# A fused forward and backward kernel on one core: value products placed earlier in the forward chain, and another order of loads and half chunks in the tail

## The chip, the cores and the metric

The kernel runs on one core of a Trainium2 chip. A core has a matrix engine (PE, with weight loads listed apart as PEld), VectorE (DVE), ScalarE (ACT), GpSimd (POOL) and SyncE (SP); each takes its own instructions in order, and they meet through semaphores. DMAs are issued from SP and from POOL. The metric is the device time of one execution in microseconds, as a median of several runs. The profile is one more execution, recorded instruction by instruction.

## The reference

The reference runs a transformer block forward and then takes the gradients of everything against a given `grad_out`. The attention goes through 64 segments of 32 tokens in turn. Each segment has 8 memory rows in front, which are the first 8 output rows of the segment before it:

```python
for s in range(n_seg):
    h = jnp.concatenate([mem, xs], axis=1)
    q, k, v = (einsum('btd,dhe->bhte', h, W) for W in (Wq, Wk, Wv))
    p = softmax(where(mask, q @ k.T * scale, -1e9))
    o = einsum('bhte,hed->btd', p @ v, Wo)
    mem = o[:, :M]
    outs.append(o[:, M:])
h = x + attention(layernorm(x)); out = h + (silu(hn @ Wg) * (hn @ Wu)) @ Wd
```

There are 2048 tokens of width 448, 16 heads of 256, and a hidden width of 1792. The outputs are `out` and the gradients of `x`, of the first memory, of Wq, Wk, Wv and Wo, and of the three weights of the gated layer. The memory makes the forward pass a recurrence over segments, and the backward pass one in the other direction.

## The kernel before

The kernel has four stages, one after the other: `forward_chain` (lines 359 to 810), `ffn_phase` (813), `backward_chain` (1032) and `tail_phase` (1289). They share a few large buffers in on-chip memory (`W`, `A`, `B`), cut by hand into tiles, so that a tile of one stage comes free only when the stage before has read it for the last time. PSUM has eight banks: five that go round under one name (`psf` in the profile), two (`fx`) and one (`po`, used as `ph` in the tail).

The order of instructions on an engine is made by a planner. It takes an instruction that it believes to be ready, those of higher rank first, and rank follows the order of the code. Code inside `k.prio.crit()` ranks above the rest. `tc.issue_after(x)` places an instruction behind `x` on its own engine. So an instruction that is written later can stand earlier in an engine's queue if, by the planner's reckoning, nothing of higher rank was ready there.

**A segment of the forward chain.** Queries and keys come first (`qk_rows`, L535 and L539, and their transposes, L549), then the scores of two halves of the heads (L622, L628) with a softmax each (L635 to L642 on DVE, the exponential on ACT, L637). Values are made in four banks. `value_rows(b)` (L652) does the three full chunks of the contraction for a bank, and `value_rest(b0)` (L660) does the last half chunk for two banks and copies both to on-chip memory, for the second pair one by ACT and one by DVE, the latter behind the end of the second softmax. `transposed_p(b)` (L671) turns the probabilities of half `b` and copies them. `values(b)` (L684) multiplies values and probabilities; its first four heads' columns are copied by DVE and the others by ACT, the token columns to `xblk` and then the memory columns. `out_proj` (L697) sums over all 32 column blocks in the bank `po`; the memory rows of the next segment come out of it (L728 to L738). `values(0)` reads the value banks 0 and 1, `values(1)` banks 2 and 3. `rest_unit` (L464) is work for later segments, laid behind `out_proj` in most segments.

**The tail.** It computes the weight gradients as sums over token blocks: 16 blocks of 128 tokens and, for the attention, 4 blocks with memory rows, 20 in all. For the gradient of Wo (`rows_by_d`, L1397) it goes through the blocks in the order 16 to 19 and then 15 down to 0. The stationary side is `X_o` (a tile a block, loaded by `outs(i0, i1, c0, c1)` for the blocks at places `i0` to `i1` of that order and the columns `c0` to `c1`), the moving side is `DCt`, gathered by `grads`. `grads(0)` issues four loads for the memory blocks (L342) and eight for the rest (L346, L347), and `grads(1)` four more (L349). `grads(0)` and the first `outs` are issued on SP in the last segment of the backward chain.

Then follow the gradients of Wv, Wk and Wq, in two halves each: six calls of `att`, and after the first and the third of them an `up_grad` for the two up-projections (16 blocks). Each makes two passes of `d_by_e` over its blocks, with seven accumulating banks: six for the three full chunks of the 448 rows (L1375), and one for the last 64 rows (the half chunks, L1380), which go to the two halves of the array by turns. With `frees` true the half chunks come after every four blocks; with `frees` false, in the first pass, all come at the end of the pass. In the first pass of `att` the four memory blocks are made on the way: a fetch from `M_v`, `M_k` or `M_q` on POOL (L1340), a pack by DVE and ACT (L1345, L1347), and a turn by PE (L1354) with copies. `k.last_mm` is the PE instruction behind which such a turn is placed. The last product (gradient of the down-projection) reads `GO`, a copy of `grad_out` that POOL loads (L1471) to the place where `DCt` and then `HN` lay before.

Of the kernel before, what the change touches and what calls it, by code (L numbers as in the profile page):

```python
# [15 lines left out]
P = 128  # L16
# [297 lines left out]
class _TailLoads:  # L314
# [18 lines left out]
    def grads(self, part):  # L333
        k, D, S, NT, M, SEG = self.k, self.k.D, self.k.S, self.k.NT, self.k.M, self.k.SEG
        sync, DHb = k.nc.sync, k.dr["DHb"]
        dcx = DHb[0:S, 0:D].rearrange("(t r i) d -> r i t d", r=4, i=SEG)
        dcm = DHb[S:, 0:D].rearrange("(t r m) d -> r m t d", r=4, m=M)
        dc8 = DHb[0:S, 0:D].rearrange("(g s i) d -> g s i d", s=16, i=SEG)
        if part == 0:
            for g in range(k.NB - NT):  # L340
                with k.tc.issue_after(k.last_load.ins):
                    sync.dma_start(out=self.DCt[:, NT + g], in_=dc8[g, :, 0:M])  # L342
        for r in range(4):
            if part == 0:
                with k.tc.issue_after(k.last_load.ins):
                    sync.dma_start(out=self.DCt[32 * r:32 * r + 24, :NT], in_=dcx[r, M:SEG])  # L346
                    sync.dma_start(out=self.DCt[32 * r + 24:32 * r + 32, 4:NT], in_=dcm[r, :, 4:NT])  # L347
            else:
                sync.dma_start(out=self.DCt[32 * r + 24:32 * r + 32, 0:4], in_=dcm[r, :, 0:4])  # L349
# [9 lines left out]
def forward_chain(k: _K):  # L359
    nc, tc = k.nc, k.tc  # L360
# [246 lines left out]
    for s in range(NSEG):  # L607
# [9 lines left out]
        with k.prio.crit():  # L617
# [29 lines left out]
            def value_rows(b):  # L647
                pV[b] = k.ps1()
                for kc in range(KC - 1):
                    for g in range(2):  # L650
                        n = 4 * g + b
                        nc.tensor.matmul(pV[b][64 * g:64 * g + 64, 0:512], lhsT=hT_flat[:, kc, sl * L:sl * L + 64],  # L652
                                         rhs=Wv_sb[:, kc, n * 512:(n + 1) * 512],
                                         start=(kc == 0), stop=False, skip_group_check=True)

            def value_rest(b0, held=None):
                for g in range(2):
                    for e in range(2):
                        m = 2 * g + b0 // 2
                        nc.tensor.matmul(pV[b0 + e][64 * g:64 * g + 64, 0:512], lhsT=hT_flat[64 * e:64 * e + 64, KC - 1, sl * L:sl * L + 64],  # L660
                                         rhs=Wv3[64 * e:64 * e + 64, m * 512:(m + 1) * 512],
                                         start=False, stop=True, skip_group_check=True)
                for e in range(2):
                    with tc.issue_after(held.ins) if held is not None and e == 1 else nullcontext():
                        k.evac(Vs[:, (b0 + e) * 512:(b0 + e + 1) * 512], pV[b0 + e][:, 0:512], "s" if held is None else "sv"[e])
# [11 lines left out]
            def values(b):  # L677
                for x in range(2):
                    po = k.ps1()
                    for hh in range(2):  # L680
                        h = HB * b + 2 * x + hh
                        for dc in range(DC):
                            i = 2 * hh + dc
                            nc.tensor.matmul(po[:, i * 2 * L:(i + 1) * 2 * L], lhsT=Vs[:, (2 * h + dc) * P:(2 * h + dc + 1) * P],  # L684
                                             rhs=PT_bd[:, h, :, :].rearrange("p g n -> p (g n)"), start=True, stop=True)
                    v = po[:, 0:8 * L].rearrange("p (j n) -> p j n", n=L)
                    j0 = 16 * b + 8 * x
                    k.evac(xblk[:, j0:j0 + 8, r * SEG:(r + 1) * SEG], v[:, :, M:L], "vs"[x])
                    k.evac(orr[:, j0:j0 + 8, :], v[:, :, 0:M], "vs"[x])
# [24 lines left out]
            value_rows(2)  # L714
            transposed_p(0)
            value_rows(3)
            value_rest(2, p_in)
            if end:
                k.fl.at(1)
            values(0)  # L720
            transposed_p(1)
            out_proj(0, 8)
            values(1)
# [308 lines left out]
def backward_chain(k: _K):  # L1032
# [98 lines left out]
    for s in range(NSEG - 1, -1, -1):  # L1131
# [12 lines left out]
        with k.prio.crit():  # L1144
# [25 lines left out]
                                         start=(dc == 0), stop=(dc == DC - 1), skip_group_check=True)  # L1170
            if s == 0:
                k.tl.grads(0)
                k.tl.outs(0, 7, 0, 6)
            pD3 = pD[:, 0:8 * L].rearrange("p (h n) -> p h n", n=L)
            prod = k.f32("f2", 8 * L, "prod")[:].rearrange("p (h n) -> p h n", n=L)
            nc.vector.scalar_tensor_tensor(out=prod, in0=pD3, scalar=k.scale, in1=P_sb, op0=ALU.mult, op1=ALU.mult)
# [112 lines left out]
def tail_phase(k: _K):  # L1289
# [72 lines left out]
    tl.outs(0, NB, 11, 16)  # L1362
    xo = tl.x

    def d_by_e(lhs_of, rhs_of, nblk, widths, store, at=None, frees=True):

        pa = accs(7)
        for b0 in range(0, nblk, 4):
            for fn in (at or {}).get(b0, ()):
                fn()  # L1370
            for b in range(b0, min(nblk, b0 + 4)):
                for kc in range(KC - 1):
                    for g in range(2):
                        w = widths[g]
                        k.last_mm = nc.tensor.matmul(pa[2 * kc + g][:, 0:w], lhsT=lhs_of(b)[:, kc * P:(kc + 1) * P], rhs=rhs_of(b, g),  # L1375
                                         start=(b == 0), stop=(b == nblk - 1), skip_group_check=True)
            for b in range(b0, min(nblk, b0 + 4)) if frees else range(nblk) if b0 + 4 >= nblk else ():
                for g in range(2):
                    w = widths[g]
                    k.last_mm = nc.tensor.matmul(pa[6][64 * g:64 * g + 64, 0:w], lhsT=lhs_of(b)[:, (KC - 1) * P:D], rhs=rhs_of(b, g),  # L1380
                                     start=(b == 0), stop=(b == nblk - 1), skip_group_check=True)
        for i in range(6):
            kc, g = divmod(i, 2)
            res = resbuf()
            evac(res[:, 0:widths[g]], pa[i][:, 0:widths[g]])
            store(kc, g, res[:, 0:widths[g]])
        res = resbuf()
        for g in range(2):
            evac(res[64 * g:64 * g + 64, 0:widths[g]], pa[6][64 * g:64 * g + 64, 0:widths[g]])
            store(KC - 1, g, res[64 * g:64 * g + 64, 0:widths[g]])  # L1390
# [29 lines left out]
    def att(hi, mem, after):  # L1420
        nm, oi, hf = halves[hi]
        o2 = OUT[oi].rearrange("d h e -> d (h e)")
        xt = load_x(nm, hf)
        for g in range(NG):
            xt[NT + g] = ring()
        for q in range(2):
            at = {}
            if q == 0:
                (f0, p0, t0), (f1, p1, t1), (f2, p2, t2), (f3, p3, t3) = mem
                at = {0: [p0, f2], 4: [lambda: t0(xt[NT]), p1, f3], 8: [lambda: t1(xt[NT + 1]), p2],  # L1430
                      12: [lambda: t2(xt[NT + 2]), p3], 16: [lambda: t3(xt[NT + 3])]}
            elif after is not None:
                at = {12: [after[0][0], after[1][0]]}

            def st(kc, g, r, q=q, hf=hf, o2=o2):
                e0 = (16 * g + 8 * hf + 4 * q) * P
                nc.gpsimd.dma_start(out=o2[kc * P:min(D, (kc + 1) * P), e0:e0 + 512], in_=r)  # L1437

            def rhs(b, g, q=q, xt=xt):
                return xt[b].rearrange("p (cl g n) -> p cl g n", g=2, n=P)[:, 4 * q:4 * q + 4, g, :]  # L1440
            d_by_e(lambda b: HC[:, b, :], rhs, NB, (512, 512), st, at, q == 1)

    def up_grad(nm, oi, after):
        xt = []
        for t in range(NT):
            x_t = ring()
            nc.sync.dma_start(out=x_t[:, 0:F], in_=dr[nm][t * P:(t + 1) * P, :])
            xt.append(x_t)
        for p0 in (0, 1024):
            ws = (512, min(512, F - p0 - 512))  # L1450

            def st(kc, g, r, p0=p0, oi=oi):
                f0 = p0 + 512 * g
                nc.gpsimd.dma_start(out=OUT[oi][kc * P:min(D, (kc + 1) * P), f0:f0 + r.shape[-1]], in_=r)

            def rhs(b, g, p0=p0, ws=ws, xt=xt):
                return xt[b][:, p0 + 512 * g:p0 + 512 * g + ws[g]]
            d_by_e(lambda b: HN[:, b, :], rhs, NT, ws, st, {8: [after[0][0], after[1][0]]} if p0 else None, p0 > 0)

    mems = [load_m(nm, hf) for (nm, _, hf) in halves] + [None]  # L1460
    mems[0][0][0]()
# [1 line left out]
    for hi in range(len(halves)):  # L1463
        att(hi, mems[hi], mems[hi + 1] if hi not in (0, 2) else None)
        if hi == 0:
            nc.gpsimd.dma_start(out=HN[:, 0:NT, :], in_=dr["HN"].rearrange("(t p) d -> p t d", p=P))
            up_grad("DGP", 7, mems[1])
        if hi == 2:
            up_grad("DU", 8, mems[3])
            GO = W(0, NB, D)  # L1470
            nc.gpsimd.dma_start(out=GO[:, 0:NT, :], in_=GO2.rearrange("(t p) d -> p t d", p=P))  # L1471

# [44 lines left out]
```

## Time and profile before

| What | Value |
|---|---|
| Median of 4 runs | 3096.22 us (3091.14 to 3101.26) |
| Profiled execution, its own time | 3088.07 us |
| Its span | 3086.3 us |
| PE busy | 2900.9 us, 94% of the span |
| DVE, ACT, POOL busy | 43%, 36%, 22% |
| PE busy from 0 to 1031.6 us (forward) | 933.7 of 1031.6 us |
| PE busy from 2399.9 us to the end (tail) | 653.1 of 686.4 us |
| Granted PE clock, mean | 0.991 |

In a timeline a row gives the start in microseconds from the start of the span, the duration, the engine, the line, the operation with the tile that it writes and the tiles that it reads, and the number of like instructions merged. In square brackets stands the time that the engine had been idle, and what it had waited for. A line number can be that of a helper: every copy out of PSUM is L75 (DVE) or L76 (ACT), and is told apart by its tiles and shape. Durations of matmuls overlap, so a rate is better read from the starts.

### The profile page before, as it was taken

What the parts mean: (1) busy time and instruction counts of PE and PEld (TensorE: products, weight loads), DVE (VectorE), ACT (ScalarE), POOL (GpSimd) and SP (SyncE); (2) the same over time, 40 slices, a digit from 0 to 9 for tenths busy, and PEclk for the clock granted to TensorE, in tenths of its full rate; (3) what the DMA queues carried; (4) which work ended last, traced back from release to release, by engine and by line L of the source; (5) the groups of instructions that cost most, each with busy time, mean ns of one, the idle gap of its engine ahead of it and who ended that gap; (6) DMA issues with size and microseconds to landing.
All of it is one profiled execution on the core that took longest, in us unless ns stands there. A gap on an engine that the chain in (4) does not pass through costs nothing.

```text
span 3086.3 us, 108337 instructions
## 1 busy us (share of the span) xinstructions
PE 2900.9 (94%) x47640; PEld 1737.6 (56%) x47650; DVE 1332.0 (43%) x3381; ACT 1114.9 (36%) x2634; POOL 673.3 (22%) x1507
## 2 busy tenths in 40 slices
PE   5899999999998999989999999999999899999999
PEld 3555555555554556666666666666666454444444
DVE  4555555555555577744444444444444001111110
ACT  2444444444444445433444344434444011111110
POOL 2222222222222222421221112212212111212111
PEclk9999999999999999989999999999999899999999
DMA  7566766766766999874554445545545998969951
GB/s 244 136 170 180 183 166 174 187 170 174 191 178 184 286 221 228 222 273 122 154 136 136 133 138 134 154 129 147 132 131 148 295 261 229 187 187 219 177 162 51
DMA packets 739468, 550.12 MB, mean 178 GB/s; under 512 B 600052, under 2 KB 635364, under 8 KB 736564
## 3 DMA queue, kind: packets, MB, share of 16 engines
q1 hardware_dynamic: 687956, 389.65, 51.8%
q0 software_dynamic: 51040, 153.54, 14.9%
q8 instruction: 374, 6.13, 0.8%
q14 instruction: 98, 0.80, 0.1%
HBM read 168.01 MB, written 234.23 MB: 130 GB/s over the span
## 4 chain that ended last, share of the span: by engine, by line
PE 65%; issue 15%; DMA 7%; DVE 6%; ACT 3%; POOL 3%; SPq 1%; POOLq 0%; ACTq 0%; DVEq 0%
PE po L1200 7%; PE psf L1151 7%; PE psf L535 6%; PE psf L652 5%; PE po L697 4%; PE psf L890 4%; PE psf L1128 4%; PE fx L1264 3%; PE fx L464 2%; PE fx L1014 2%; PE psf L1222 2%; DVE arA L75 2%; PE psf L549 2%; PE psf L1160 2%; PE psf L1397 2%
## 5 line engine op out<-in xcount | busy, mean ns | idle before, releaser
L75 DVE CAST arA<-psf 128x256 bf16<-128x256 f32 (+3 forms) x933 | 427.8, 479 | 782.4 <-PE psf L1375 233.6
L76 ACT CAST arA<-psf 128x96 bf16<-128x96 f32 (+5 forms) x915 | 353.4, 409 | 1011.5 <-PE psf L1375 254.7
L1200 PE MATMUL po<-arW,arA 128*32 128x448 bf16 x6144 | 347.8, 356 | 4.2 <-DMA arW<-Tq 2.7
L1375 PE MATMUL psf<-arW,arA 128*128 128x512 bf16 x980 | 249.6, 382 | 0.0
L1375 PEld LDWEIGHTS <-arA 128*128 128x128 bf16 x1440 | 137.0, 98 | 167.1 <-issue 18.0
L1151 PEld LDWEIGHTS <-arW 128*128 128x128 bf16 x8192 | 213.2, 96 | 24.8 <-issue 24.8
L1151 PE MATMUL psf<-arA,arW 128*128 128x40 bf16 x8192 | 216.6, 180 | 6.2 <-DVE arA L1226 5.1
L1200 PEld LDWEIGHTS <-arA 128*32 128x32 bf16 x6144 | 152.1, 96 | 115.7 <-ACT arA L76 9.2
L652 PE MATMUL psf<-arW,arA 128*64 128x512 bf16 x1536 | 216.4, 382 | 0.0
L535 PE MATMUL psf<-arW,arA 128*32 128x512 bf16 x3072 | 192.5, 383 | 12.5 <-DVE arA L738 12.5
L76 ACT CAST arB<-psf 128x64 bf16<-128x64 f32 (+3 forms) x384 | 122.0, 318 | 151.3 <-PE psf L539 108.1
L697 PE MATMUL po<-arW,arA 128*32 128x256 bf16 (+1 forms) x4096 | 141.3, 263 | 10.9 <-DVE arA L75 7.7
L890 PE MATMUL psf<-arW 128*128 128x256 bf16 (+1 forms) x1288 | 146.3, 274 | 1.3 <-DVE arA L956 0.7
L890 PEld LDWEIGHTS <-arW 128*128 128x128 bf16 (+1 forms) x1344 | 102.4, 97 | 51.5 <-issue 40.8
L1397 PE MATMUL psf<-arW 128*128 128x448 bf16 x525 | 113.2, 358 | 11.7 <-DMA arW<-X_o 11.7
L1161 ACT COPY arA<-psf 128x1024 bf16<-128x1024 bf16 x128 | 123.3, 1015 | 1.8 <-PE psf L1160 0.4
L1128 PEld LDWEIGHTS <-arW 128*128 128x128 bf16 x2048 | 86.4, 99 | 61.9 <-issue 57.7
L535 PEld LDWEIGHTS <-arA 128*32 128x32 bf16 x3072 | 70.2, 96 | 89.2 <-DVE arA L738 18.0
L76 ACT COPY arA<-psf 128x512 bf16<-128x512 bf16 (+3 forms) x142 | 84.4, 595 | 87.3 <-DVE arA L75 77.3
L464 PE MATMUL fx<-arA,arW 128*128 128x64 bf16 (+1 forms) x2048 | 84.8, 196 | 32.2 <-ACT arB L76 19.0
L697 PEld LDWEIGHTS <-arA 128*32 128x32 bf16 x4096 | 93.6, 96 | 33.0 <-DVE arA L75 11.1
L1437 POOL DMA_DIRECT2D out_dram<-arA x96 | 51.9, 547 | 272.6 <-DVE arA L75 272.1
(286 smaller groups left out, 4624.9 us busy)
## 6 DMA issues: line engine op xcount, KB each, us to landing
arW<-T SPq DMA_DIRECT2D x256, 128.0 KB
X_o<-arA SPq DMA_DIRECT2D x37, 512.0 KB
T<-arA SPq DMA_DIRECT2D x64, 256.0 KB
X_v<-arA POOLq DMA_DIRECT2D x32, 512.0 KB, 5.0
X_k<-arA POOLq DMA_DIRECT2D x32, 512.0 KB, 3.9
X_q<-arA POOLq DMA_DIRECT2D x32, 512.0 KB, 3.2
out_dram<-arA POOLq DMA_DIRECT2D x90, 128.0 KB, 4.1
VG<-arA SPq DMA_DIRECT2D x64, 160.0 KB
```

The costliest lines, as they stand in the source:

```text
L75: return nc.vector.tensor_copy(out=out, in_=in_)
L76: return nc.scalar.copy(out=out, in_=in_)
L464: nc.tensor.matmul(banks[w][:, i * 64:(i + 1) * 64], lhsT=lhsT, rhs=xr[lo:hi, kc, :], start=(kc == 0 and i == 0), stop=(kc == KC - 1), ski ...
L535: nc.tensor.matmul(banks[w][32 * q:32 * q + 32, :], lhsT=hT_roll[:, kc, sl, M:L], rhs=(Wq_sb, Wk_sb)[w][:, kc, col(q, b)], start=(kc == 0) ...
L652: nc.tensor.matmul(pV[b][64 * g:64 * g + 64, 0:512], lhsT=hT_flat[:, kc, sl * L:sl * L + 64], rhs=Wv_sb[:, kc, n * 512:(n + 1) * 512], sta ...
L697: nc.tensor.matmul(pO[32 * q:32 * q + 32, 0:w], lhsT=xblk[:, j, r * SEG:(r + 1) * SEG], rhs=Wo_sb[:, cj(j), 256 * dh:256 * dh + w], start= ...
L890: nc.tensor.matmul(ps[fp][:, f2 * 256:(f2 + 1) * 256], lhsT=Wt[lo:hi, kc, c * P:(c + 1) * P], rhs=xT[lo:hi, kc, :], start=(kc == 0 and f2 ...
L1128: nc.tensor.matmul(ps[b][:, i * 2 * L:(i + 1) * 2 * L], lhsT=lhs[:, at, :], rhs=rhs_bd[:, cl // 2, :, :].rearrange("p g n -> p (g n)"), st ...
L1151: nc.tensor.matmul(pss[b][:, jj * L:(jj + 1) * L], lhsT=WoT_sb[:, kc, c * P:(c + 1) * P], rhs=do_roll[:, kc, sl, :], start=(kc == 0), stop ...
L1200: nc.tensor.matmul(pH[32 * (j % 4):32 * (j % 4) + 32, 0:D], lhsT=blk[nm][:, j, r * SEG:(r + 1) * SEG], rhs=WT[:, cj(j), :], start=(nm == " ...
L1375: k.last_mm = nc.tensor.matmul(pa[2 * kc + g][:, 0:w], lhsT=lhs_of(b)[:, kc * P:(kc + 1) * P], rhs=rhs_of(b, g), start=(b == 0), stop=(b = ...
L1397: k.last_mm = nc.tensor.matmul(pa[i][:, 0:D], lhsT=lhs_of(b, i), rhs=rhs_of(b), start=(bi == 0), stop=(bi == m + 3))
```

## The change

Three things change in the tail and one in the forward chain.

In the last backward segment, `grads(0)` now issues the first four `X_o` loads itself, between its four loads for the memory blocks and its eight others; the call after it loads places 4 to 7 only. In `d_by_e` the switch `frees` is gone: half chunks follow every four blocks in every pass, and `k.last_mm` is set by half chunks only. The load of `GO` is written behind the fourth call of `att` and no longer ahead of it. In the forward chain `values(0)` is called ahead of `value_rest(2, p_in)` and no longer behind it.

```diff
@@ grads(self, part), part == 0
             for g in range(k.NB - NT):
                 with k.tc.issue_after(k.last_load.ins):
                     sync.dma_start(out=self.DCt[:, NT + g], in_=dc8[g, :, 0:M])
+            self.outs(0, k.NB - NT, 0, 6)
@@ forward_chain, a segment
             transposed_p(0)
             value_rows(3)
+            values(0)
             value_rest(2, p_in)
             if end:
                 k.fl.at(1)
-            values(0)
             transposed_p(1)
             out_proj(0, 8)
             values(1)
@@ backward_chain, last segment
                 k.tl.grads(0)
-                k.tl.outs(0, 7, 0, 6)
+                k.tl.outs(4, 7, 0, 6)
@@ d_by_e
-    def d_by_e(lhs_of, rhs_of, nblk, widths, store, at=None, frees=True):
+    def d_by_e(lhs_of, rhs_of, nblk, widths, store, at=None):
...
-                        k.last_mm = nc.tensor.matmul(pa[2 * kc + g][:, 0:w], ...
+                        nc.tensor.matmul(pa[2 * kc + g][:, 0:w], ...
-            for b in range(b0, min(nblk, b0 + 4)) if frees else range(nblk) if b0 + 4 >= nblk else ():
+            for b in range(b0, min(nblk, b0 + 4)):
                 for g in range(2):
@@ att and up_grad
-            d_by_e(lambda b: HC[:, b, :], rhs, NB, (512, 512), st, at, q == 1)
+            d_by_e(lambda b: HC[:, b, :], rhs, NB, (512, 512), st, at)
@@ tail_phase, the loop over halves
         if hi == 2:
             up_grad("DU", 8, mems[3])
+        if hi == 3:
             GO = W(0, NB, D)
             nc.gpsimd.dma_start(out=GO[:, 0:NT, :], in_=GO2.rearrange("(t p) d -> p t d", p=P))
```

More of the change, by code (lines that the diff above doesn't have):

```diff
@@ L1374, in d_by_e @@
                         w = widths[g]
-                        k.last_mm = nc.tensor.matmul(pa[2 * kc + g][:, 0:w], lhsT=lhs_of(b)[:, kc * P:(kc + 1) * P], rhs=rhs_of(b, g),
+                        nc.tensor.matmul(pa[2 * kc + g][:, 0:w], lhsT=lhs_of(b)[:, kc * P:(kc + 1) * P], rhs=rhs_of(b, g),
                                          start=(b == 0), stop=(b == nblk - 1), skip_group_check=True)
-            for b in range(b0, min(nblk, b0 + 4)) if frees else range(nblk) if b0 + 4 >= nblk else ():
+            for b in range(b0, min(nblk, b0 + 4)):
                 for g in range(2):
@@ L1457, in rhs @@
                 return xt[b][:, p0 + 512 * g:p0 + 512 * g + ws[g]]
-            d_by_e(lambda b: HN[:, b, :], rhs, NT, ws, st, {8: [after[0][0], after[1][0]]} if p0 else None, p0 > 0)
+            d_by_e(lambda b: HN[:, b, :], rhs, NT, ws, st, {8: [after[0][0], after[1][0]]} if p0 else None)
     mems = [load_m(nm, hf) for (nm, _, hf) in halves] + [None]
```

## The prediction

> **What bounds the kernel now.** I read the page first, then the engine timelines of one forward segment, then the tail. On the page PE is busy 94% of the span and carries the chain that ended last:
>
> ```profile
> PE 65%; issue 15%; DMA 7%; DVE 6%; ACT 3%; POOL 3%; SPq 1%; POOLq 0%; ACTq 0%; DVEq 0%
> ```
>
> So only time in which PE waits, or PE work itself, can move the end. The forward chain (64 segments, to about 1031 us) is a recurrence: each segment needs the memory rows of the last. PE's timeline of one segment (start, duration, what):
>
> ```profile
> 503.65 0.82 PE L652 MATMUL psf<-arW,arA 128*64 128x512 bf16 x6
> 504.40 0.41 PE L660 MATMUL psf<-arW,arA 64*64 64x512 bf16 x4
> 504.74 0.46 PE L684 MATMUL psf<-arB,arW 128*128 128x80 bf16 x8
> 505.50 0.28 PE L671 MATMUL fx<-ident,arB 128*40 128x40 bf16 x8 [0.30 <-DVE arB L642]
> 506.24 0.22 PE L464 MATMUL fx<-arA,arW 128*128 128x64 bf16 x2 [0.46 <-ACT arB L76]
> 506.44 0.62 PE L697 MATMUL po<-arW,arA 128*32 128x256 bf16 x16
> 506.99 0.46 PE L684 MATMUL psf<-arB,arW 128*128 128x80 bf16 x8
> ```
>
> PE waits 0.76 us here: for the second softmax (L642), then for the copies of `values(0)` that `out_proj(0, 8)` (L697) reads. DVE over the same time:
>
> ```profile
> 504.56 0.32 DVE L639 TENSOR_REDUCE ssum<-S_sb 128x4 f32<-128x160 f32 x1 [0.27 <-ACT S_sb L637]
> 505.12 0.33 DVE L642 TENSOR_TENSOR arB<-S_sb,rs 128x160 bf16<-128x160 f32 x1
> 505.37 0.69 DVE L75 CAST arW<-psf 128x512 bf16<-128x512 f32 x1
> 505.97 0.42 DVE L75 CAST arA<-psf 128x256 bf16<-128x256 f32 x1
> 506.43 0.30 DVE L75 CAST arB<-fx 40x160 bf16<-40x160 f32 x1
> ```
>
> DVE is full from 504.56 to 506.73. The 0.69 copy (a value bank) stands before the 0.42 copy, which ends at 506.39; L697 starts at 506.44. In the tail PE has three large waits, and the half chunks (L1380) show what grouping costs:
>
> ```profile
> 2411.63 2.05 PE L1397 MATMUL psf<-arW 128*128 128x448 bf16 x5 [11.74 <-DMA arW<-X_o]
> 2554.60 1.01 PE L1354 MATMUL ph<-ident,arB 128*128 128x128 bf16 x8 [6.02 <-DVE arW L75]
> 2683.51 4.51 PE L1380 MATMUL fx<-arW,arA 128*64 128x512 bf16 x40
> 2693.24 1.05 PE L1380 MATMUL fx<-arW,arA 128*64 128x512 bf16 x8
> 2848.40 1.01 PE L1354 MATMUL ph<-ident,arB 128*128 128x128 bf16 x8 [6.25 <-DVE arW L75]
> ```
>
> The last wait is in truth one for a DMA behind POOL's load of GO (L1471), as POOL and DVE show:
>
> ```profile
> 2832.79 1.19 POOL L1471 DMA_DIRECT2D arW<-in_grad_out_dram x1
> 2834.79 0.78 POOL L1340 DMA_DIRECT2D arA<-M_k x1 [0.81 <-DMA out_dram<-arA]
> 2847.32 0.43 DVE L1345 COPY arA<-arA 128x1024 bf16<-128x1024 bf16 x1 [11.46 <-DMA arA<-M_k]
> 2847.67 0.68 DVE L75 COPY arW<-ph 128x1024 bf16<-128x1024 bf16 x1
> ```
>
> GO lands 12.8 us after its issue, at 2845.6; M_k behind it 12.5 us after its own. The pack (L1345) waits, and the copy that PE needs stands behind it on DVE.
>
> [...] in a second pass four blocks take 6.27 us (2687.95 to 2694.22), 24 main matmuls of 0.2158 us take 5.18, so eight half chunks cost 1.09; in the run of 40 they cost 4.54, 0.108 each plus about 0.22 for the two switches. [...] here matmuls after 2848 take 0.43 us instead of 0.216. [...]
>
> **The change part by part.**
>
> *Half chunks back to every four blocks (first passes).* Six attention passes of 20 blocks: 5 x 1.09 - 4.54 = +0.91 each; two up-projection passes of 16 blocks: 4 x 1.09 - 3.68 = +0.68 each. Sum +6.8 us, on PE. What is bought: in a first pass the third group comes 2 x 1.09 = 2.18 later, while M loads land. The waits of 6.02 (first attention pass), 0.39 and 0.65 (second and sixth) become 3.84, 0 and 0; the slow clock after the first (matmuls from 2554.60 to 2558.03 took 1.25 more than at 0.216) should mostly go[...]. Together -4.4, bounds -2 and -5. Transposes are still placed after the last PE instruction of the group before, so their place is the same.
>
> *GO.* One POOL DMA, 1.19 us of issue, moves in the code past two M_k fetches, two M_q fetches and 16 stores of the fourth attention pass. The planner doesn't keep code order on POOL: HN (L1466, written after the first pass) ran at 2536.75, before that pass's fetches at 2538.45. So GO need only wait till nothing of higher rank is ready. The M_k fetches need packs that ended on ACT at 2831.69 and 2832.64, before POOL was free at 2832.79: I place both ahead of GO. M_k then lands in about 8 us as in other passes (8.2 in the second), that is 2843; its consumer comes at 2842.1 + 2.2 (2841.12 plus four matmuls, plus the two groups). The 6.25 wait goes, and 2.8 of slow clock (2848.40 to 2854.69, 3.47 us of work). Gain 9.1. If GO stays ahead, or lands ahead of the fifth pass's fetches, a wait of 6.25 - 2.18 = 4.1 remains: gain 5. GO itself is wanted only at 3036.
>
> *Loads.* On SP four X_o loads move before eight DCt loads, whose issues ran from 2385.98 to 2399.3. The first four products need only these X_o and the first four DCt loads, so they can run at about 2400, under the wait. The next needs all of DCt, now 768 KB later: some 2414 instead of the first product at 2411.63, still at the slow clock. In the kernel before block five ran at 2418.94; at 2.2 us a block for three blocks the eighth runs near 2420.5 instead of 2422.35. Gain 2; 0 if the last memory rows of DCt (L349, issued 2426.91) then hold the end of the pass, 4.5 at most (four products of 1.13). I take 1.5.
>
> Tail: +6.8 - 4.4 - 9.1 - 1.5 = -8.2.
>
> *values(0) ahead of value_rest.* Nothing is added. P's copies end at 504.29, the third bank's main chunks at about 504.42, so `values(0)` can start where L660 did. Its first copy was ready 0.35 after the start (506.99 to 507.34 in the second half): 504.77. Where the planner puts it on DVE decides. (a) Between ssum and rs: in early segments it fills such gaps (at 87.69 ssum, 87.93 a copy, 88.16 rs). Then the row 504.80 copy, 505.13 rs, 505.21 second copy, 505.34 L642 until 505.67; L697 from 505.27; transposes until 506.14; value bank 505.59; the PT copy 506.24 to 506.54; the second `values` at 506.59 instead of 506.99, 0.40 earlier. (c) After L642: DVE's sum is the same, the PT copy ends at 506.73, but L697 runs from 505.84, so the second `values` starts at 506.78: 0.2 earlier. (b) Ahead of ssum, DVE waits 0.21 for it, and values(1) starts at 506.9 to 507.0: 0 to 0.1. The two value banks copied later (ACT's half too) are first read by `values(1)`. What follows keeps its distance: 48 matmuls of 0.030, then the memory rows. A segment without rest units takes 15.01 us (1003.51 to 1018.52), one with them 15.02 (712.09 to 727.11) or 15.30 (510.58 to 525.88), so the chain and not PE's sum sets the period, and the gain stays. SP's stores of the value banks (506.11) and POOL's of P (505.75) come up to 0.6 later; nobody waits for them within the segment. I take 0.25 x 64 = -16; ends -26 (0.40) and +10 (0.15 lost).
>
> Sum: -16 - 8.2 = -24. The profiled run took 3088.07 (span 3086.3); it gives 3064. The four runs have a median of 3096.22 (3091.1 to 3101.3), so 3072 there.
>
> **Rivals.** (1) The planner finds P's copies late (they end only 0.13 us before the third bank's chunks) and sends the four value_rest matmuls first, as before: forward 0, tail -8, 3088. Chance 0.25. For it: that margin; against: the trace's own times. (2) Forward gain as in (a) or better, tail too: -26 - 12 = 3058. Chance 0.18. (3) Slower: DVE's queue holds the copy ahead of ssum while PE still runs value_rest first; each 0.1 us that DVE then waits beyond 0.2 costs 6.4 us. It decides from 0.47 us (0.27 x 64 = 17, which eats the tail's 8 and 9 more); all of value_rest ahead makes 0.21 + 0.34 = 0.55: +22 - 8, 3110. Chance 0.09. (4) Forward as forecast, but GO keeps ahead of M and the start gains nothing: 3096 - 16 - 2.6 = 3077, inside the forecast's own range.
>
> **How the numbers follow.** A measurement of this kernel can tell about 0.3%, 9.3 us, from no change. Forecast with (4): 0.48, own range 3064 to 3082. From 3056 (half of rival 2 below it is left out) to 3093 (rival 1 with a tail of -3) lie 8 in 10. Faster: 0.48 + 0.18 + 0.05 of rival 1 = 0.71; same 0.20; slower 0.09.
>
> **What would show it.** Right: L684 before L660 on PE, the 0.42 copy before the 0.69 one, L697's wait near nothing, segments of some 14.75 us; L1380 in eights throughout, the 6.25 wait gone, M_k ahead of GO; X_o products at 2400. Wrong: L660 still ahead of L684, or L642 later by more than 0.4 us; a new wait of 4 us in the fifth attention pass.

## The result, and the profile after

Over 36 runs beside 55 of the kernel before, the changed kernel takes 3094.18 us (3080.17 to 3112.43) against 3097.36 (3086.81 to 3126.12). The ratio is 0.9982, with a 95% interval of 0.9969 to 0.9994: some 5.6 us less, and less than the 0.3% that the prediction had called measurable. The forecast was 24 us, and its range ended at 3093. The profiled execution has a span of 3081.9 us against 3086.3.

The page of the changed kernel, busy times and then the chain that ended last:

```profile
PE 2927.9 (95%) x47640; PEld 1735.6 (56%) x47650; DVE 1329.3 (43%) x3381; ACT 1117.6 (36%) x2634; POOL 674.7 (22%) x1507
...
PE 69%; issue 10%; DVE 7%; DMA 5%; ACT 3%; POOL 1%; SPq 1%; ACTq 0%; POOLq 0%; DVEq 0%
```

PE executes as many matmuls as before (47640), and is busy 27 us longer (2900.9 before). Most of the 27 us stands at one line: the 4096 matmuls of `out_proj` (L697 before, L698 after) are busy 141.3 us before and 166.0 after, with means of 263 and 264 ns. So these matmuls didn't become longer. What this is can be read from the forward chain. PE's timeline of a segment after (lines from L343 on are one higher than before):

```profile
513.43 0.45 PE L685 MATMUL psf<-arB,arA 128*128 128x80 bf16 x8
513.81 0.41 PE L661 MATMUL psf<-arW,arA 64*64 64x512 bf16 x4
514.44 0.29 PE L698 MATMUL po<-arW,arA 128*32 128x256 bf16 x3 [0.22 <-DVE arA L75]
514.68 0.27 PE L672 MATMUL fx<-ident,arB 128*40 128x40 bf16 x8
...
515.72 0.45 PE L685 MATMUL psf<-arB,arA 128*128 128x80 bf16 x8
```

and DVE's:

```profile
513.90 0.18 DVE L642 RECIPROCAL rs<-ssum 128x4 f32<-128x4 f32 x1
514.00 0.39 DVE L75 CAST arA<-psf 128x256 bf16<-128x256 f32 x1
514.31 0.32 DVE L643 TENSOR_TENSOR arB<-S_sb,rs 128x160 bf16<-128x160 f32 x1
```

`values(0)` (L685) stands ahead of `value_rest` (L661), and the 0.39 copy lies between the reciprocal and L643: case (a) of the prediction. The two waits of 0.30 and 0.46 us are one of 0.22.

`out_proj` itself is now cut up. In a segment without rest unit its rows before are

```profile
984.36 0.62 PE L697 MATMUL po<-arW,arA 128*32 128x256 bf16 x16 [0.66 <-DVE arA L75]
985.30 1.50 PE L697 MATMUL po<-arW,arA 128*32 128x256 bf16 x48
```

and after

```profile
964.87 0.29 PE L698 MATMUL po<-arW,arA 128*32 128x256 bf16 x3 [0.23 <-DVE arA L75]
965.30 0.83 PE L698 MATMUL po<-arW,arA 128*32 128x192 bf16 x22
966.52 1.50 PE L698 MATMUL po<-arW,arA 128*32 128x192 bf16 x39
```

The same 64 matmuls show 2.12 us before and 2.62 after, and 39 of them take as long as 48 did. Within the last row the eighth starts 0.32 us after the seventh, at 966.96, just after DVE's copy of `values(1)` ends (966.90). More of `out_proj` now runs ahead of `values(1)` (25 matmuls instead of 16), so less is left to fill the time until that copy. A matmul lasts 0.25 to 0.28 us in this view, so most of such a pause counts as busy time: part of the waiting was moved to where the busy figures don't show it.

The segments didn't become 0.25 us shorter everywhere. The view of busy time by stretch, for a segment without rest unit and one with it (columns: stretch, its length, busy PE, PEld, DVE, ACT, POOL with instruction counts, granted clock, DMA share, GB/s), of the kernel before, with one of its longer segments as a third row:

```profile
973.49:988.50 15.01, 12.78 (x246) 6.67 (x246) 7.60 (x24) 6.39 (x16) 3.29 (x10) 1.00 0.78 199
204.34:219.36 15.02, 13.95 (x278) 7.74 (x279) 7.97 (x24) 6.76 (x17) 3.23 (x10) 1.00 0.48 126
327.85:344.38 16.53, 16.52 (x291) 8.93 (x288) 7.87 (x24) 6.76 (x17) 2.88 (x8) 1.00 0.80 185
```

and the same three of the kernel after:

```profile
954.97:969.72 14.75, 13.19 (x246) 6.79 (x246) 7.44 (x23) 6.40 (x16) 3.31 (x10) 1.00 0.70 203
212.53:227.41 14.88, 14.25 (x278) 7.77 (x278) 7.84 (x24) 6.78 (x17) 4.50 (x14) 1.00 0.80 195
320.67:337.38 16.71, 16.69 (x286) 9.02 (x286) 8.09 (x24) 6.77 (x17) 2.62 (x9) 1.00 0.81 181
```

A bare segment gains 0.26 us, one with a rest unit 0.14, and the third sort, whose PE is full in both kernels, loses 0.18. In this third sort runs the product `px`: after every 16th segment the memory rows of 16 segments (`mblk`) are multiplied with Wo, 32 matmuls of 448 columns (L778 before, L779 after) into one of the two `fx` banks. It has low rank, and the planner lays it out in short runs over the next segments: before, in runs of 4, 2 and 2 a segment, the last of them in the fourth segment; after, in runs of 2, 3 and 2, so that two matmuls are left for a fifth.

Periods come from the starts of a segment's first L535 (L536 after). Here and below the kernel's second segment is counted as segment 0 and its last as segment 62, which leaves out the very first one; that makes 62 periods:

| Segments | Before, us | After, us | Difference |
|---|---|---|---|
| first 5 | 83.18 | 80.79 | -2.39 |
| 35 plain ones with rest unit | 527.01 | 521.69 | -5.32 |
| 15 with `px` (and the one that follows it) | 242.55 | 250.95 | +8.40 |
| last 7, without rest unit | 105.06 | 103.37 | -1.69 |
| all | 957.80 | 956.80 | -1.00 |

The five segments of a `px` took 80.7 to 81.1 us before and 83.3 to 84.1 after, 5.8 and at least 8.9 us above five plain ones. Of the 3.1 us more, each counted above the plain segment of its own kernel, about 0.3 lie in each of the first three segments, 0.9 in the fourth (16.04 before, 16.81 after) and 1.3 in the fifth (15.07 and 16.25). In the fifth the two matmuls that are left stand in the middle of the queries and keys, and PE then waits for a copy:

```profile
355.28 0.55 PE L779 MATMUL fx<-arW,arA 128*128 128x448 bf16 x2
356.15 0.83 PE L536 MATMUL psf<-arW,arA 128*32 128x512 bf16 x12 [0.31 <-DVE arA L75]
```

Beside this 1.00 us, another 3.6 us in which the changed execution is ahead lie before the first of these starts (60.7 us before, 57.2 after). In the other executions below that start lies anywhere from 57.7 to 61.5 us with the old order and from 57.1 to 61.7 with the new one, so this isn't the change's.

The tail, from the end of the backward chain to the end, is 0.8 us shorter. PE's waits for turned memory rows (the transposes at L1354 before, L1355 after) are now:

```profile
2551.28 1.01 PE L1355 MATMUL ph<-ident,arB 128*128 128x128 bf16 x8 [4.05 <-DVE arW L75]
2666.61 0.91 PE L1355 MATMUL ph<-ident,arB 128*128 128x128 bf16 x8 [2.27 <-DVE arW L75]
2847.02 0.61 PE L1355 MATMUL ph<-ident,arB 128*128 128x128 bf16 x8 [0.46 <-DVE arW L75]
```

First passes of the six attention calls took 41.69, 34.79, 34.33, 43.49, 34.34 and 35.05 us before, and 40.74, 39.25, 35.24, 35.78, 35.23 and 35.23 after. The fourth call gains 7.71, the second loses 4.46.

### The profile page after: what moved, and what is told of

Its sections match the earlier page's. It is cut to its first block, busy times and chain, and to the rows that moved or that the text cites. A ratio compares the mean times of both kernels' runs of the same rounds, so it can differ in the third digit from the quotient of the medians.

```text
span 3081.9 us, 108379 instructions
## 1 busy us (share of the span) xinstructions
PE 2927.9 (95%) x47640; PEld 1735.6 (56%) x47650; DVE 1329.3 (43%) x3381; ACT 1117.6 (36%) x2634; POOL 674.7 (22%) x1507
## 4 chain that ended last, share of the span: by engine, by line
PE 69%; issue 10%; DVE 7%; DMA 5%; ACT 3%; POOL 1%; SPq 1%; ACTq 0%; POOLq 0%; DVEq 0%
PE po L1201 7%; PE psf L1152 7%; PE psf L536 6%; PE psf L1376 5%; PE po L698 5%; PE psf L653 4%; PE psf L891 4%; PE psf L1129 4%; PE fx L1265 3%; DVE arA L75 2%; PE fx L1015 2%; PE psf L1223 2%; PE psf L550 2%; PE psf L1161 2%; PE psf L1398 2%
## 5 line engine op out<-in xcount | busy, mean ns | idle before, releaser
L536 PE MATMUL psf<-arW,arA 128*32 128x512 bf16 x3072 | 192.4, 382 | 13.4 <-DVE arA L739 12.5
L698 PE MATMUL po<-arW,arA 128*32 128x256 bf16 (+1 forms) x4096 | 166.0, 264 | 14.2 <-DVE arA L75 11.6
L698 PEld LDWEIGHTS <-arA 128*32 128x32 bf16 x4096 | 99.9, 96 | 46.0 <-DVE arA L75 29.9
L536 PEld LDWEIGHTS <-arA 128*32 128x32 bf16 x3072 | 70.3, 96 | 93.1 <-DVE arA L739 21.4
L1129 PE MATMUL psf<-arB,arW 128*128 128x80 bf16 x2048 | 96.6, 201 | 13.5 <-DVE arB L1182 4.3
```

The source lines that it names most:

```text
L536: nc.tensor.matmul(banks[w][32 * q:32 * q + 32, :], lhsT=hT_roll[:, kc, sl, M:L], rhs=(Wq_sb, Wk_sb)[w][:, kc, col(q, b)], start=(kc == 0) ...
L698: nc.tensor.matmul(pO[32 * q:32 * q + 32, 0:w], lhsT=xblk[:, j, r * SEG:(r + 1) * SEG], rhs=Wo_sb[:, cj(j), 256 * dh:256 * dh + w], start= ...
L1129: nc.tensor.matmul(ps[b][:, i * 2 * L:(i + 1) * 2 * L], lhsT=lhs[:, at, :], rhs=rhs_bd[:, cl // 2, :, :].rearrange("p g n -> p (g n)"), st ...
```

## The experiments

The theory going in, A: the waits that the move of `values(0)` removed on PE had held other work (`px`, rest units), which now takes time of its own. Its rival, B: the forward gain is there, and the tail ate it.

**One part alone.** The first kernel is the kernel before with

```diff
             value_rows(3)
+            values(0)
             value_rest(2, p_in)
...
-            values(0)
```

and nothing else; the second is the changed kernel with these lines put back.

> The kernel before with values(0) ahead of value_rest alone, the tail untouched. Theory A (filler): the waits that the move removes on PE had held the products px of the last memory rows with Wo and the rest units; with the waits gone that work takes PE time of its own, so the start of segment 62 comes only 1 to 3 us earlier beyond what start-up differs, plain segments fall by 0.12 to 0.26 us and the five segments after each px by +0.1 to +1.2 us dearer; time -1 to -4 us. Theory B (the forward gain is there and the tail ate it): the forward part ends 8 us or more earlier and the time falls by 8 to 16 us.

> The changed kernel with value_rest put back ahead of values(0): the three edits of the tail alone. Theory A (filler): forward segments as before (15.01 us, 16.53 after px), and the tail, from the start of its first Wo product to the end, within 1.5 us of before (-0.8 in the changed kernel's profile); time -2 to +1 us. Theory B: the tail alone is 5 us or more slower than before, which would hide a forward gain of that size.

The move alone: ratio 0.9999 (0.9979 to 1.0020); segment 62 starts 956.49 us after segment 0, 1.3 us less than before, with the same periods as in the changed kernel (14.88, 14.75, 16.71 to 16.97 with `px`, and 16.24 in the fifth segment after it began). The tail alone: ratio 0.9967 (0.9951 to 0.9984), 10 us less, with the old periods. So B falls: the tail gave, and the forward part did not. The tail gave more than A had said (its profile shows 4.5 us); the spread of its waits, further down, makes that understandable.

**Without `px`.** Does `px` take the gain back? Its loop was cut from `range(MC)` to `range(1)`, in the kernel before and with the move. These two leave out part of the output.

> The kernel before with the product px of a block of last memory rows with Wo cut to one matmul of 32 (the other 31 are left out, so that part of the output is not computed). Theory A (filler): PE does px partly in its own waits: the five segments after each group of 16 fall from 16.5 us towards 15.0, the forward part becomes shorter by about 5.8 us for each of three groups, 17 us in all, plus what the blocks after the forward part save. Theory B (px cost nothing on the path, all in waits): the forward part changes by less than 5 us.

> The same cut of px (31 of 32 matmuls left out, that part of the output not computed) with values(0) ahead of value_rest. Against the cut kernel without the move, theory A (filler: px takes back what the move gains): with nothing to take it back the move is worth 0.12 to 0.26 us in nearly every one of 64 segments, 8 to 14 us at the start of segment 62. Theory B (the move is worth little for another reason, such as the recurrence setting the period by another path): the difference stays at 1 to 3 us.

Segment 62 starts 941.56 us after segment 0 without the move, and 929.79 with it. The move is then worth 11.8 us, in the times 9.6 us (medians 3071.77 and 3062.15; ratios to before 0.9911 and 0.9872, intervals 0.9875 to 0.9946 and 0.9842 to 0.9901). With `px` it is worth 1.0 to 1.3. Cutting `px` saves 16.2 us before and 26.7 with the move, and its 96 matmuls in the three groups need only 96 x 0.19 = 18.2 us on PE (0.19 from the kernel before, where the 32 of the last `px` start at 1033.55 us and what follows them at 1039.60). So `px` was covered a little by waits before, and with the move costs more than its own work. A, which only takes cover away, doesn't reach that.

**`px` in one run.** Two things were left: the pieces, and the bank that they hold for five segments. Ranking `px` with the chain puts the 32 matmuls in one run:

```diff
-            px = k.fx1()
-            for j in range(MC):
-                nc.tensor.matmul(px[:, 0:D], ...)
-            k.evac(orow, px[:, 0:D], "v")
+            with k.prio.crit():
+                px = k.fx1()
+                for j in range(MC):
+                    nc.tensor.matmul(px[:, 0:D], ...)
+                k.evac(orow, px[:, 0:D], "v")
```

> values(0) ahead of value_rest, and the 32 matmuls of px ranked with the chain, so that they stand on PE in one run of 32 between two segments and not in runs of 2 and 3 over five segments; the tail as before. Theory P (pieces: px costs 8.9 us per group of 16 there because it is cut into runs of 2 and 3 between PE's other shapes and because its bank of fx, one of two, is held for five segments): a group then costs its own 32 x 0.19 = 6.1 to 6.5 us in one segment, the next four are plain 14.88, and segment 62 starts 7 to 9 us earlier than with the move alone (relative to segment 0). Theory S (PE's plain sum: px takes what its matmuls need wherever they stand): no more than 1 us of difference.

> The kernel before with px in one run of 32, values(0) behind value_rest as it was. Before, px cost 5.8 us per group with the waits helping to hide it. Theory P: one run of 32 costs 6.1 to 6.5 us and the waits of 0.76 to 1 us per segment hide nothing of it, so segment 62 starts 1 to 2 us later than in the kernel before, and the move is then worth about 8 us between this kernel and the one with both. Theory S: the same as before within 1 us.

With the move a group costs 5.82 us (one segment of 20.70, then 14.88 again), and segment 62 starts 948.10 us after segment 0: 8.4 us better than the move alone, 9.7 better than before; ratio 0.9947 (0.9920 to 0.9973). Without the move a group costs 5.91 us and segment 62 comes at 959.39, 1.6 us later than before; ratio 1.0012 (0.9992 to 1.0032). Theory P stands: the move is worth 11.3 us between these two.

**The bank, held by hardly any work.** Here `px` is cut to two matmuls, the second placed four segments after the first; part of the output is left out again, and each kernel ran once:

```diff
-            for j in range(MC):
-                nc.tensor.matmul(px, mblk[:, j], ...)
-            k.evac(orow, px[:, 0:D], "v")
+            nc.tensor.matmul(px, mblk[:, 0], ..., stop=False)
+        if end or (jm == 3 and s > 16):
+            with tc.issue_after(pm_t.ins) if not end else nullcontext():
+                nc.tensor.matmul(px, ident, ..., stop=True)
+            k.evac(orow, px[:, 0:D], "v")
```

> With values(0) ahead of value_rest, px cut to two matmuls of 32 (the other 30 are left out, and the second multiplies the identity, so that part of the output is not computed), the second placed four segments after the first: the bank of fx is held as long as by the whole px, with hardly any PE work. It tells apart what theory P lumps. If the held bank is the cost, segments 16 to 19 of each group take 0.8 us or more above the plain 14.88; if it is PE's work in pieces, they take 14.9 to 15.1.

> The kernel before with px cut to two matmuls (30 of 32 left out, the second multiplies the identity, so that part of the output is not computed), the second four segments after the first: the bank of fx held, hardly any PE work. With the move the same hold cost 1.16 us a segment (16.04 against 14.88). Theory H (the move made the held bank expensive: the second transposes and the rest unit now stand closer together and want both banks at once): here the hold costs 0 to 0.5 us, 15.0 to 15.5. Rival W (the hold costs the same either way, and what the move lost is the cover of waits for px's own matmuls): 16.0 to 16.2 here too.

With the move the four segments take 16.04, 16.19, 16.04 and 16.04 us. The timeline of one shows why:

```profile
332.37 0.27 PE L671 MATMUL fx<-ident,arB 128*40 128x40 bf16 x4
332.57 0.94 PE L697 MATMUL po<-arW,arA 128*32 128x256 bf16 x25
333.47 0.25 PE L671 MATMUL fx<-ident,arB 128*40 128x40 bf16 x4
...
334.16 0.45 PE L684 MATMUL psf<-arB,arA 128*128 128x80 bf16 x8
```

`transposed_p` writes to both `fx` banks (rows 0 to 39 of one, 64 to 103 of the other). With one of them taken it runs as four and four, well apart, and `values(1)` (L684) comes 12.05 us into the segment instead of 11.17. Without the move the four segments take 15.83 to 16.03 against 15.01. A group's hold is then 4.9 us with the move and 3.7 without. The measurement lies between theory H (0 to 0.5 a segment) and rival W (1.0 to 1.2), nearer to W. So of the 3.1 us that a group took back, about 1.2 (4.9 - 3.7) are the bank in the first four segments. These two kernels hold it no longer than that, and their fifth segments are nearly plain (14.95 and 15.07). The fifth segment of the whole `px` accounts for another 1.3. What remains, 0.6, would be matmuls that lost their cover. This is a subtraction that takes the parts to add up; no run shows it by itself.

**GO alone, half chunks alone.** Each is the kernel before with one edit of the tail.

> The kernel before with the load of GO alone moved behind the fourth pass. My account: M_k's fetches go ahead of it on POOL, the wait of 6.25 us in the fourth attention pass falls to 2.6 us or less (its half chunks still come in one run of 44, so 2.2 us less cover than in the changed kernel), the slow clock after it goes or shrinks, and that pass takes 36 to 38.5 us instead of 43.5: 5 to 7.5 us off the time. Rival: GO keeps its place or another load holds M_k: the wait stays at 4 us or more and the gain is under 3 us.

> The kernel before with half chunks in fours in every pass of the tail, nothing else. The price is sure: 0.91 us in each of six attention passes and 0.68 in each of two others, 6.8 us. By the prediction's account the waits give back 4.4, so +2.4 us. By the cushion account (waits for transposed rows vary from run to run; the kernel before drew 13.3 us of them in its profile, other runs of the same tail 14 to 33) it gives back more than it costs: 0 to -6 us.

With GO's load moved, both M_k fetches stand ahead of it on POOL, as predicted. The wait is still 4.07 us, and the pass still met the slow clock after it: ACT's copy of the next turned rows began 1.11 us after DVE's copy had ended (2855.92 to 2857.03). In the kernel before that distance is 1.10, with transposes of 1.01 us and a granted clock of 0.54 over 2848.40 to 2854.69; in the changed kernel, with transposes of 0.61 and a granted clock of 1.00 over 2847.02 to 2850, it is 0.70. The pass took 41.32 us instead of 43.49, where 36 to 38.5 had been expected. These are the numbers of the rival (a wait of 4 us or more, a gain under 3), in this one execution: GO left its place, but the fetches landed 12.1 and 14.6 us after their issue all the same. Half chunks in fours: ratio 0.9995 (0.9977 to 1.0014), between the two accounts and not told apart by it; the waits in its profile sum to 7.3 us against 13.3.

The waits for turned rows vary far more from run to run than the prediction assumed from one profile. In eight profiled executions with the tail untouched (the kernel before, the move alone, and the six kernels with an altered `px` so far) the waits for turned rows over 0.25 us sum to 13.3, 33.7, 14.6, 17.6, 22.7, 17.9, 17.5 and 21.5 us, 19.9 on average; the one in the fourth pass was 3.5 to 18.2. The kernel before, in its profile, had drawn the least. In three executions with the tail of the change (the third in the next experiment) they sum to 6.8, 4.3 and 13.4, 8.2 on average. That is 11.7 less for 6.8 us of half chunks, a net 4.9 before any slow clock, and so fits the tail's measured 10 us (5 to 15) better than the 0.8 us of one pair of profiles. Which edit of the tail brings it is not settled: half chunks alone gave 1.5 us (from 7 gained to 4 lost), and these few profiles differ in more than that edit.

**Together.** The changed kernel with `px` in one run, and the same forward part with GO alone.

> The changed kernel with px in one run of 32. If the pieces and the held bank of px were what took the forward gain back, it is 8 to 9 us faster than the changed kernel, 14 us (10 to 18) faster than before: ratio 0.9955 (0.994 to 0.997). If the tail's draws decide instead, it lies within 4 us of the changed kernel: ratio about 0.998.

> values(0) ahead of value_rest, px in one run, and GO moved; half chunks at the end of a first pass and the order of the X_o loads as before. By the prediction's own sums half chunks in fours cost 6.8 us and return 4.4, so this one should be 1 to 4 us faster than the changed kernel with px whole. If the tail's waits vary from run to run as they do in the traces so far (0.5 to 18 us in the fourth pass), the earlier half chunks are a cushion worth more than their price, and this one is 2 to 6 us slower than that kernel and spreads more.

The first: 3079.84 us, ratio 0.9939 (0.9923 to 0.9955), 19 us (14 to 24) below the kernel before, just past the good end of what was expected. The second: 3080.78, ratio 0.9945 (0.9930 to 0.9960). The two differ in half chunks and in the order of the `X_o` loads, and that difference is neither a gain nor a loss that these runs can tell.

**What holds the M fetches.** In the changed kernel POOL issues, and DVE packs:

```profile
2836.05 0.77 POOL L1341 DMA_DIRECT2D arB<-M_k  x1
2837.94 1.16 POOL L1473 DMA_DIRECT2D arW<-in_grad_out_dram  x1 [1.13 <-DMA out_dram<-arA]
```

```profile
2850.08 0.43 DVE L1346 COPY arB<-arB 128x1024 bf16<-128x1024 bf16 x1 [3.11 <-DMA arB<-M_k]
```

GO now stands behind both fetches. Still the second is used only 14.0 us after its issue (the first 10.7); in the two kernels of the last pair it was 22.0 and 20.9, and the fourth pass waited 6.39 and 9.09 us with GO moved. The last two kernels take the load away from all fetches:

```diff
+                k.last_fetch = nc.gpsimd.dma_start(out=ld, ...)
...
-        if hi == 3:
+        if hi == 5:
             GO = W(0, NB, D)
-            nc.gpsimd.dma_start(out=GO[:, 0:NT, :], ...)
+            with tc.issue_after(k.last_fetch.ins):
+                nc.gpsimd.dma_start(out=GO[:, 0:NT, :], ...)
```

the first of them with all of the change, `px` in one run, and HN's load behind its own pass's fetches in the same way.

> The changed kernel with px in one run, GO's load behind the last fetch of transposed memory rows (M) of the tail and HN's load behind the four M_v fetches of the first pass. Theory L (a load of 1.8 MB issued within 2 us of an M fetch makes that fetch land 14 to 22 us after its issue, whichever of the two fetches stands next to it; alone one takes 4 to 6): the second M_k fetch of the fourth pass, 14.0 to 22.0 us with GO right behind it, lands within 8 us, the waits of 4 to 5 us in the first and up to 6.4 in the fourth pass fall below 1.5, and the time is 3 to 10 us below the same kernel without these two moves: ratio to before 0.991 to 0.993. Rival V (the M fetches vary from run to run for another reason, stores or the X loads): landings of 14 us and more stay, the ratio stays at 0.994.

> The kernel before with GO's load behind the last M fetch of the tail, nothing else. Theory L: both M_k fetches of the fourth pass land within 8 us of their issue and the wait there, 6.25 us in the kernel before and 4.07 with GO moved to right behind the fetches, goes to 0 to 1 us; the fourth pass takes 34.3 to 36 us. Rival V: a wait of 3 us or more is left.

The kernel before with GO last: ratio 0.9975 (0.9958 to 0.9992), no wait over 0.25 us left in the fourth pass. That is 7.7 us less (2.5 to 13.0) with one edit, where half chunks alone gave 1.5. So GO is the likelier source of the tail's 10 us, though this is not the place that the change gave it. POOL and DVE there:

```profile
2843.08 0.77 POOL L1340 DMA_DIRECT2D arB<-M_k  x1
...
2855.58 0.43 DVE L1345 COPY arB<-arB 128x1024 bf16<-128x1024 bf16 x1 [4.29 <-DMA arB<-M_k]
```

The first fetch took 5.4 us, but the second 12.5 with neither of the two large loads near it on POOL's queue, and the fifth pass waited 5.96. In the kernel with everything the two fetches took 9.7 and 10.4 us, where theory L had expected less than 8. With GO right behind them the second fetches took 14.0 to 22.0 us in five executions, so GO looks like one cause of late fetches, but two executions without it are few, and it isn't the only cause: theory L and its rival V both hold in part. The kernel with everything has no wait over 0.25 us for turned rows, takes 3070.69 us and has a ratio of 0.9908 (0.9873 to 0.9943) to before. Of the kernels that compute the whole output it is the fastest, some 29 us below the kernel before. The interval overlaps that of the same kernel without the moves of GO and HN (0.9923 to 0.9955), so the worth of these moves stays open.

## Why the prediction was wrong

**The step that failed is "so the chain and not PE's sum sets the period, and the gain stays".** It compared segments with and without rest units, found 15.01 us for both, and concluded that PE had room to spare in all 64. How much room was left it didn't count: 2.2 us of waits in a bare segment, 1.0 with a rest unit. And it applied the answer to every segment, where 12 of the 57 periods after the first five took 16.0 to 16.7 us, with PE busy for 16.52 of 16.53 in the one shown. The profile of before held this row. The move's gain, 0.25 us a segment, was right where PE had room: 0.26 without rest unit, and the second `values` starts 11.17 us into the segment instead of 11.42. That this size was met is partly luck: 0.25 stood between several cases, the case that came was (a), and for (a) the prediction had 0.40. With a rest unit 5.3 instead of 8.8 us were won over 35 segments. In the segments of `px` 8.4 us were lost where 3.8 were to be won. That this work in pieces, the `fx` bank that it holds, and the two pieces pushed into a fifth segment would cost more once the segment is tighter was nowhere in the sum. Without `px` the move is worth 11.8 us, with `px` in one run 11.3, with `px` in pieces 1.0 to 1.3.

**Nothing is added.** No instruction was, but PE's busy time in a bare segment rose from 12.78 to 13.19 us for the same 246. The waits fell by 0.7 us there, and only 0.26 of them shortened the segment. The rest is mostly the pauses inside `out_proj` that the view counts as busy, 2.62 us instead of 2.12 for its 64 matmuls. So waits that go from the list are not all time that is won.

**The order on DVE.** Right, as case (a). No rival about the planner came true. The second `values` came 0.25 us earlier in the segment, not 0.40: PE began it 0.14 us after the copy that it waits for, behind 25 matmuls of `out_proj`.

**Half chunks.** The price was right: 0.91 and 0.89 in the third and fifth attention pass, 0.68 in each up-projection. The 0.22 us for two switches can be read from the starts in the kernel before: the first half chunk starts 0.31 us after the main matmul ahead of it (2683.20 to 2683.51), where main matmuls are 0.216 apart, and the next main matmul 0.98 us after the first of eight half chunks, which at 0.108 take 0.86. The wait of the first pass became 4.05, where 3.84 was forecast. That the slow clock would then mostly go was the author's estimate (no wait of that length stands in the tail of before), and it was wrong: the 15 matmuls from that wait on took 3.32 us at a granted clock of 0.57, against 3.21 at 0.59 in the kernel before.

**GO.** The order on POOL and the fourth pass were right in this execution, -7.71 us against the +0.91 - 9.1 = -8.2 of the sum. "The 6.25 wait goes" was right by luck of a draw: with GO in that place the wait was 0, 0.46, 4.07, 6.39 and 9.09 us in five executions. The second pass, where the sum had a wait of 0, drew 2.27 us and slow clock (0.53 granted over 2666.61 to 2670.24). The sum took a fetch at 8 us, but in the profile of before the fetches that a pack waited for were used 5.7 to 16.9 us after their issue.

**Loads.** Taken as 1.5 us, worth 0. Four products ran at 2393 to 2399 us, and the fifth block was 4.4 us earlier in the stage. The slow clock, which had fallen on the first three blocks (0.59 granted over 2411.63 to 2418.50), now fell on the fifth and sixth (2.21 and 1.65 us instead of 1.13; 0.56 granted over 2410.92 to 2414.59), and PE waited 1.14 and 1.42 us for later `X_o` loads. Together this gave all of it back: the stage took 135.97 us against 135.88.

**The sum.** Forward -16 against -1.0 by the trace and -0.3 by the times of the part alone (-6.5 to +6.2). Tail -8.2 against -0.8 in the profile, but -10 (-15 to -5) over the runs of the part alone. So 15 of the missing 18 us are the forward step. The two parts alone add up to some 11 us, and the whole measured 5.6 (1.9 to 9.6); the intervals overlap, and no run explains the difference.

## What to carry to other kernels

Before a gain is multiplied by the number of rounds, list the period of every round: those that differ show which work fills the waits, and whether PE is full there. A wait on the critical engine may be the cover of low-ranked work. Here that work cost more than its matmuls when it was cut into pieces and kept one of the two `fx` banks all the while, and one run of it was cheaper once the waits had gone. When a wait disappears from the list, see whether the segment became shorter by as much. Sizes of waits for DMAs from a single profile are draws (0 to 9.09 us for one of them here); ask for several before pricing their removal.

## What the runs showed of the hardware

Waits of 2.27 and 4.05 us (the changed kernel) and of 2.90 us (half chunks alone) were followed at once or nearly so by matmuls at 0.43 us a piece instead of 0.216. After waits of 4.08 us (half chunks alone) and 4.34 us (the tail alone) that began about 1 us later. Among waits of 2 to 3 us the length did not decide it: in the kernel before, a wait of 2.20 us (to 1345.47) was followed by a granted clock of 0.50 over the next 2 us, and one of 2.28 us (to 1108.39) by 1.00; with GO last, matmuls after a wait of 2.17 us (to 2675.18) came at 0.216 us. So a wait below the 3.84 us of the forecast was no protection from the slow clock.

A fetch of 512 KB on POOL's queue was used 5 to 26 us after its issue, by a pack that waited for it, in executions of nearly the same program (5.1 in the changed kernel with `px` in one run, issued at 2651.42; 25.8 with the move alone, issued at 2844.44). The spans of one kernel also went with the mean granted clock: of the runs of the kernel before in the first set of experiments, 17 at 0.988 averaged 3100.4 us and the two at 0.991 averaged 3091.1. Which of the two is cause and which effect these runs don't tell.
